# Attention scores and values in another layout, one transfer per q, k and v, and GpSimd's work of the first block given to VectorE

## The chip, the cores and the metric

The kernel runs on one NeuronCore of a Trainium2 chip. The metric is the device time of one execution in microseconds (us). Its engines are called by the names of the profile: PE (TensorE, matrix products; PEld is its weight loads), DVE (VectorE), ACT (ScalarE), POOL (GpSimd) and SP (SyncE, which issues the transfers here).

## The reference

Three stages follow each other. Local attention over chunks of 64 rows, then two feed-forward layers with different activations:

```python
B, H, S, D = q.shape                  # 4, 8, 576, 64
scores = scale * q_c @ k_c.T          # inside chunks of 64
attn = exp(scores - max) / (sum + 1e-9)
x = (attn @ v_c)  -> (B*S, H*D)       # 2304 tokens x 512
h = x @ w_in;  x = (h * sigmoid(1.702 * h)) @ w_out      # 512 -> 2048 -> 512
h = x @ w_in2; x = (h * tanh(softplus(h))) @ w_out2      # 512 -> 2048 -> 512
```

q, k and v are float32. The four weight matrices are float64, and the kernel reads them as pairs of 32-bit words.

## The kernel before, in words

**Tiling.** The 2304 tokens are 18 attention tiles of 128 tokens (two chunks of 64). Three tiles make a block of 384 tokens, so there are six blocks (j). The hidden width of 2048 is 16 slices (f). A step n is one slice of one block. In a step of the first layer `in_proj` (line 347) makes the hidden slice in 12 matrix products, ACT applies the activation (`gelu`, line 359), and `out_a` (line 374) adds the slice of two steps earlier to the block's output in 12 products.

**High and low parts.** Every product is made of three: each operand is split into a high part (the value rounded to the short form that PE reads fast) and a low part (the value minus its high part). `mm3` (line 342) multiplies high by high, high by low and low by high. So each weight piece, each hidden slice and each x needs one cast for the high part and one subtraction for the low part.

**Weights of the first layer.** There are 32 pieces of 512 KB (16 of w_in, 16 of w_out), in the order in which the first block needs them. Each goes through four operations, which `Weights` (lines 75 to 186) holds: `load` (SP, into one of 5 buffers), `scale` (ACT, line 141), `join` (DVE, lines 151 and 152, which make one float32 of two words), `split` (ACT casts the high part, line 173; POOL subtracts for the low part, line 174). A buffer can be filled again once the subtraction has read it. `convert` (line 177) does one of each for successive pieces, twice per step while the first block lasts. The pieces stay in memory for the other five blocks. The second layer's weights are joined during the first layer, written out, and split when the second layer begins, with the subtraction on POOL.

**Attention.** A tile goes through `load` (q, k, v), `transposes` (PE), copies of both (ACT or DVE), `scores` (PE), `shift` (DVE: maximum at line 277, subtraction at line 278), `exp` (ACT), `sums` (DVE, lines 291 to 293), `normalize` (line 297; POOL in the first block, DVE later), `attn_t` (PE), a copy (ACT), `pv` (PE), `x_hi` (ACT) and `x_lo` (DVE). `scores` and `pv` are 16 products of 64 by 64 per tile. They are placed on quarters of the 128 by 128 array: the partitions of the operands choose the rows, those of the result the columns. q and k come in two transfers per tile and v in four, so that two heads of a pair and two chunks lie where the products want them.

**Order.** All engines take their instructions in the order in which the program writes them. The first three tiles and steps 0 to 3 follow a list written by hand (`PLAN`, line 24): a letter is an operation, the number its tile or step. "w" is a number of idle products that keep PE busy. From step 4 on the loop at line 539 writes each step; in it tile 4 and tile 5 are made in the first block, one attention operation group per step. Within a step the order is `in_proj`, one `convert`, `gelu`, `g_hi`, `g_lo` (the hidden slice's own split; in the first block its subtraction is on POOL, line 370), attention, `out_a`, the other `convert`.

Of the kernel before, what the change touches and what calls it, by code (L numbers as in the profile page):

```python
# [9 lines left out]
F32 = mybir.dt.float32  # L10
F32R = mybir.dt.float32r
AF = mybir.ActivationFunctionType
ALU = mybir.AluOpType
# [3 lines left out]
P = 128  # L17
# [18 lines left out]
def tile_kernel(  # L36
# [40 lines left out]
    class Weights:  # L77
# [8 lines left out]
        def __init__(self, w_in, w_out, staged):  # L86
# [5 lines left out]
            self.raw, self.f32, self.hi, self.lo = {}, {}, {}, {}  # L92
            self.first, self.ahead = 0, NRAW - 2 if staged else NRAW
# [33 lines left out]
        def load_ahead(self):  # L127

            used = self.at["join" if self.staged is not None else "split"]
# [36 lines left out]
        def split(self):  # L166
# [7 lines left out]
            nc.gpsimd.tensor_tensor(out=lo, in0=w, in1=hi.bitcast(F32), op=ALU.subtract)  # L174
            self.hi[key], self.lo[key] = hi, lo

        def convert(self):
# [35 lines left out]
    def load_values(t, i):  # L213

        for c in range(2):
            b, s = divmod(i * P + c * CH, S)
            for r in range(2):
                nc.sync.dma_start(
                    out=t[r * CH : (r + 1) * CH].rearrange("k (p c d) -> k p c d", c=2, d=D)[:, :, c],
                    in_=v[b, r * NP : (r + 1) * NP, s : s + CH, :].rearrange("p k d -> k p d"),  # L220
                )

    class Attention:
# [31 lines left out]
        def scores(self):  # L255
            self.pt = pt = self.psum("sc")
            for p in range(NP):
                for c in range(2):
                    c0 = p * P + c * CH
                    cs = slice(c * CH, (c + 1) * CH)  # L260
                    for r in range(2):
                        rs = slice(r * CH, (r + 1) * CH)
                        nc.tensor.matmul(
                            pt[cs, r, p * CH : (p + 1) * CH],
                            self.qt[rs, c0 : c0 + CH],
# [191 lines left out]
    with tc.manual_schedule():  # L457
# [193 lines left out]
```

## Time and profile before

| what | us |
|---|---|
| median of 3 runs (lowest, highest) | 895.48 (894.75, 896.47) |
| the profiled execution's own time | 894.35 |
| its span in the profile | 892.4 |
| PE busy / DVE busy / ACT busy / POOL busy | 869.9 / 355.6 / 276.8 / 115.0 |

The span is the time from the first to the last recorded instruction. PE's busy time is the union of its matrix products, whose ends are modelled, so that products that overlap count once. Share of the span tells little here, because the first 110 us have another limit than the rest; the rows below are therefore taken by stretch.

### The profile page before, as it was taken

To read this page: it belongs to the slowest core of one execution; us is meant where nothing else is said; L and a number is where in the kernel's file an instruction comes from. 1 tells how busy PE (TensorE), PEld (TensorE's weight loads), DVE (VectorE), ACT (ScalarE), POOL (GpSimd) and SP (SyncE) were. 2 spreads that over 40 slices of the span, in tenths; PEclk is the share of its full clock that TensorE was granted. 3 is DMA by queue.
4 is the path that set the end of the run, shared out by engine and by line. 5 is a ranking of instruction groups with operands and counts; after the bars stand their busy time and mean duration, and the time that the engine had idled before them with its cause. 6 is when DMAs were issued, how large, how long until landed. Compare 5 with 4: busy or idle time off the path is not lost.

```text
span 892.4 us, 13796 instructions
## 1 busy us (share of the span) xinstructions
PE 869.9 (97%) x5724; PEld 812.1 (91%) x5724; DVE 355.6 (40%) x633; ACT 276.8 (31%) x469; POOL 115.0 (13%) x92
## 2 busy tenths in 40 slices
PE   7878999999999999999999999999999999999998
PEld 5777899999999999999999999999999999999997
DVE  5789744445445455445333222222222222222221
ACT  4777733333334343333434111111111111111111
POOL 2688700000000000000565000000000000000000
PEclk9999999999999999999999999999999999999999
DMA  8957724455336435523342000300200200200000
GB/s 208 284 163 218 213 96 107 107 139 181 117 96 195 125 107 169 153 71 128 112 127 83 1 1 1 107 1 1 106 1 1 107 1 1 107 1 1 36 1 36
DMA packets 93406, 82.69 MB, mean 93 GB/s; under 512 B 60320, under 2 KB 76704, under 8 KB 93344
## 3 DMA queue, kind: packets, MB, share of 16 engines
q1 hardware_dynamic: 93344, 81.81, 31.0%
q8 instruction: 45, 0.74, 0.3%
q14 instruction: 17, 0.14, 0.1%
HBM read 62.39 MB, written 19.40 MB: 92 GB/s over the span
## 4 chain that ended last, share of the span: by engine, by line
PE 88%; DVE 4%; DMA 3%; ACT 2%; SPq 2%; issue 1%; POOL 0%; DVEq 0%; POOLq 0%; ACTq 0%
PE h L345 14%; PE h L343 14%; PE h L344 14%; PE acc L343 7%; PE acc L344 6%; PE acc L345 6%; PE accb L435 5%; PE accb L434 5%; PE accb L433 5%; PE third L434 3%; PE third L435 2%; PE third L433 2%; DVE raw L152 2%; DVE raw L151 2%; PE tr L247 1%
## 5 line engine op out<-in xcount | busy, mean ns | idle before, releaser
L365 DVE CAST gh<-t 128x384 fp32r<-128x384 f32 x176 | 69.3, 394 | 476.0 <-ACT t L413 296.1
L343 PE MATMUL h<-xh,wi 128*128 128x384 f32 x512 | 172.0, 336 | 1.9 <-ACT t L361 1.8
L345 PE MATMUL h<-xh,wi 128*128 128x384 f32 x512 | 171.9, 336 | 0.6 <-POOL wi L174 0.6
L344 PE MATMUL h<-xl,wi 128*128 128x384 f32 x512 | 171.3, 335 | 0.0
L413 ACT ACTIVATE t<-h 128x384 f32<-128x384 f32 x96 | 47.2, 492 | 335.2 <-PE h L345 334.4
L343 PE MATMUL acc<-gh,wo 128*128 128x384 f32 x384 | 134.1, 349 | 0.0
L344 PE MATMUL acc<-gl,wo 128*128 128x384 f32 x384 | 128.6, 335 | 0.0
L345 PE MATMUL acc<-gh,wo 128*128 128x384 f32 x384 | 128.5, 335 | 0.0
L370 DVE TENSOR_TENSOR gl<-t,gh 128x384 fp32r<-128x384 f32 x176 | 98.3, 559 | 11.8
L361 ACT ACTIVATE t<-h 128x384 f32<-128x384 f32 x96 | 47.1, 491 | 172.3 <-PE h L345 81.3
L343 PEld LDWEIGHTS h<-xh,wi 128*128 128x128 f32 x512 | 96.1, 188 | 4.6 <-ACT t L361 3.2
L344 PEld LDWEIGHTS h<-xl,wi 128*128 128x128 f32 x512 | 96.1, 188 | 1.3
L345 PEld LDWEIGHTS h<-xh,wi 128*128 128x128 f32 x512 | 96.1, 188 | 0.9 <-POOL wi L174 0.9
L345 PE MATMUL h<-x2h,wi 128*128 128x384 f32 x256 | 86.4, 337 | 0.0
L343 PE MATMUL h<-x2h,wi 128*128 128x384 f32 x256 | 86.2, 337 | 0.0
L344 PE MATMUL h<-x2l,wi 128*128 128x384 f32 x256 | 86.0, 336 | 0.0
L435 PE MATMUL accb<-wo,gl 128*128 128x512 f32 x192 | 76.2, 397 | 0.0
L434 PE MATMUL accb<-wo,gh 128*128 128x512 f32 x192 | 75.8, 395 | 0.0
L433 PE MATMUL accb<-wo,gh 128*128 128x512 f32 x192 | 74.6, 389 | 0.0
L343 PEld LDWEIGHTS acc<-gh,wo 128*128 128x128 f32 x384 | 72.1, 188 | 2.0
L344 PEld LDWEIGHTS acc<-gl,wo 128*128 128x128 f32 x384 | 72.2, 188 | 0.0
L345 PEld LDWEIGHTS acc<-gh,wo 128*128 128x128 f32 x384 | 72.1, 188 | 0.0
(85 smaller groups left out, 1052.5 us busy)
## 6 DMA issues: line engine op xcount, KB each, us to landing
raw<-in_moe_w_in_dram SPq DMA_DIRECT2D x32, 512.0 KB, 4.1
raw<-in_moe_w_out_dram SPq DMA_DIRECT2D x32, 512.0 KB, 4.0
w_f<-wf SPq DMA_DIRECT2D x32, 256.0 KB, 2.2
ws<-w_f SPq DMA_DIRECT2D x32, 256.0 KB, 2.7
v<-in_v_dram SPq DMA_DIRECT2D x72, 64.0 KB, 2.9
out_dram<-o SPq DMA_DIRECT2D x18, 256.0 KB, 2.1
q<-in_q_dram SPq DMA_DIRECT2D x26, 128.0 KB, 4.2
k<-in_k_dram SPq DMA_DIRECT2D x26, 128.0 KB, 4.3
```

The lines of the kernel that those rows point to most:

```text
L151: nc.vector.tensor_scalar(lo, lo, 29, None, op0=ALU.logical_shift_right)
L152: nc.vector.scalar_tensor_tensor(to, hi, 3, lo, op0=ALU.logical_shift_left, op1=ALU.bitwise_or)
L343: nc.tensor.matmul(o, wh, mh, start=start, stop=False)
L344: nc.tensor.matmul(o, wh, ml, start=False, stop=False)
L345: nc.tensor.matmul(o, wl, mh, start=False, stop=stop)
L361: nc.scalar.activation(gt[n], hp.pop(n), AF.Gelu_apprx_sigmoid)
L365: (nc.scalar.copy if n < KF else nc.vector.tensor_copy)(gh[n], gt[n])
L370: eng.tensor_tensor(out=gl[n], in0=gt.pop(n), in1=gh[n].bitcast(F32), op=ALU.subtract)
L413: nc.scalar.activation(gt[n], h, AF.Mish)
L433: nc.tensor.matmul(o, a[:, ts], wh, start=f == 0, stop=False)
L434: nc.tensor.matmul(o, a[:, ts], wl, start=False, stop=False)
L435: nc.tensor.matmul(o, b[:, ts], wh, start=False, stop=f == KF - 1)
```

## The change

**Layout and transfers.** The heads now lie in q, k and v as they do in memory. So q, k and v of a tile are read in one transfer each (two where a tile crosses a batch). `scores` puts two neighbouring head pairs on the two halves of the result's partitions, and both chunks of a head pair side by side. `pv` takes the rows of the array by chunk and its columns by head; before, it took rows by head and columns by pair.

**Engines.** In the first layer's weights, in the hidden slices of the first block and in `normalize`, the subtraction or product that POOL did is now on DVE. POOL keeps the second layer's weights.

**Order.** A weight piece's subtraction is no longer written with its cast: it is put on a list (`open`) and written after the next piece's `join` (`rest`). A hidden slice's subtraction is written in the next step, before that step's `gelu`. `PLAN` is unchanged; its letter U now means DVE.

```diff
         def load_ahead(self):
-            used = self.at["join" if self.staged is not None else "split"]
+            used = self.at["join"] if self.staged is not None else self.at["split"] - len(self.open)
...
             nc.scalar.copy(hi, w)
-            nc.gpsimd.tensor_tensor(out=lo, in0=w, in1=hi.bitcast(F32), op=ALU.subtract)
-            self.hi[key], self.lo[key] = hi, lo
+            self.hi[key] = hi
+            self.open.append((key, w, hi, lo))
+            if self.staged is not None:
+                self.rest()
+
+        def rest(self):
+            eng = nc.vector if self.staged is None else nc.gpsimd
+            while self.open:
+                key, w, hi, lo = self.open.pop(0)
+                eng.tensor_tensor(out=lo, in0=w, in1=hi.bitcast(F32), op=ALU.subtract)
+                self.lo[key] = lo
+
+        def parts(self, key):
+            if key not in self.lo:
+                self.rest()
+            return self.hi[key], self.lo[key]
...
             if self.at["scale"] > self.at["join"]:
                 self.join()
+            self.rest()
             if self.at["load"] > self.at["scale"]:
                 self.scale()
...
-            for r in range(2):
-                nc.sync.dma_start(
-                    out=t[done : done + n].rearrange("t (p r d) -> t p r d", r=2, d=D)[:, :, r],
-                    in_=src[b, r * NP : (r + 1) * NP, s : s + n, :].rearrange("p t d -> t p d"),
-                )
+            nc.sync.dma_start(
+                out=t[done : done + n].rearrange("p (h d) -> p h d", h=H),
+                in_=src[b, :, s : s + n, :].rearrange("h p d -> p h d"),
+            )
...
-            self.v = at.tile([P, H * D], F32, tag="v", name=f"v{self.i}")
-            load_values(self.v, self.i)
+            self.v = load_tok(at, "v", v, self.i)
...
         def scores(self):
-            for p in range(NP):
+            for u in range(NP // 2):
                 for c in range(2):
-                    c0 = p * P + c * CH
-                    cs = slice(c * CH, (c + 1) * CH)
-                    for r in range(2):
-                        rs = slice(r * CH, (r + 1) * CH)
-                        nc.tensor.matmul(
-                            pt[cs, r, p * CH : (p + 1) * CH],
+                    o = (u * 2 + c) * CH
+                    for w in range(2):
+                        c0 = (2 * u + w) * P + c * CH
+                        for r in range(2):
+                            rs = slice(r * CH, (r + 1) * CH)
+                            nc.tensor.matmul(
+                                pt[w * CH : (w + 1) * CH, r, o : o + CH],
...
         def pv(self):
-                    w, o = p % 2, p // 2 * P + c * CH
-                    vs = slice((2 * p + c) * D, (2 * p + c + 1) * D)
-                    qs = slice(p * P + c * CH, p * P + (c + 1) * CH)
+                    cs = slice(c * CH, (c + 1) * CH)
                     for r in range(2):
-                        rs = slice(r * CH, (r + 1) * CH)
+                        h = 2 * p + r
+                        o = (r * NP // 2 + p // 2) * P + p % 2 * CH
                         nc.tensor.matmul(
-                            pt[w * D : (w + 1) * D, r, o : o + CH],
-                            self.v[rs, vs],
-                            self.a[rs, qs],
+                            pt[r * D : (r + 1) * D, c, p * CH : (p + 1) * CH],
+                            self.v[cs, h * D : (h + 1) * D],
+                            self.a[cs, o : o + CH],
...
     def g_lo(n):
-        eng = nc.gpsimd if n < KF else nc.vector
-        eng.tensor_tensor(out=gl[n], in0=gt.pop(n), in1=gh[n].bitcast(F32), op=ALU.subtract)
+        nc.vector.tensor_tensor(out=gl[n], in0=gt.pop(n), in1=gh[n].bitcast(F32), op=ALU.subtract)
...
-            "U": lambda i: tiles[i].normalize(pool),
-            "u": lambda i: tiles[i].normalize(nc.vector),
+            "U": lambda i: tiles[i].normalize(nc.vector),
...
                 if n < KF:
                     W[0].convert()
+                while late:
+                    g_lo(late.pop())
                 gelu(n)
                 g_hi(n)
-                g_lo(n)
+                if n < KF:
+                    late.append(n)
+                else:
+                    g_lo(n)
...
-                    att.normalize(pool if n < KF else nc.vector)
+                    att.normalize(nc.vector)
```

The order of instructions at three places. In these rows stands the line, the operation, what it writes and reads, and the size of the result; line numbers after the change are 1 to 16 higher than before.

The first place is DVE's queue while the first three tiles are finished, before step 0. raw is a weight piece, wi and wo its split parts, xl the low part of x, e the exponentials. Before:

```order
L151 TENSOR_SCALAR raw_221<-raw_221 128x512
L152 SCALAR_TENSOR_TENSOR raw_221<-raw_221 128x512
L339 TENSOR_TENSOR xl_387<-pv_315,xh_386 128x4x128
L151 TENSOR_SCALAR raw_273<-raw_273 128x512
L152 SCALAR_TENSOR_TENSOR raw_273<-raw_273 128x512
L339 TENSOR_TENSOR xl_387<-pv_348,xh_386 128x4x128
L339 TENSOR_TENSOR xl_387<-pv_398,xh_386 128x4x128
```

And after:

```order
L152 TENSOR_SCALAR raw_212<-raw_212 128x512
L153 SCALAR_TENSOR_TENSOR raw_212<-raw_212 128x512
L307 TENSOR_TENSOR e_201<-e_201,rc_237 128x512
L307 TENSOR_TENSOR e_first<-e_first,rc_275 128x512
L348 TENSOR_TENSOR xl_366<-pv_300,xh_365 128x2x4x64
L152 TENSOR_SCALAR raw_264<-raw_264 128x512
L153 SCALAR_TENSOR_TENSOR raw_264<-raw_264 128x512
L185 TENSOR_TENSOR wi_345<-raw_168,wi_345 128x512
L185 TENSOR_TENSOR wi_373<-raw_197,wi_373 128x512
L185 TENSOR_TENSOR wo_393<-raw_212,wo_393 128x512
L348 TENSOR_TENSOR xl_366<-pv_328,xh_365 128x2x4x64
L348 TENSOR_TENSOR xl_366<-pv_376,xh_365 128x2x4x64
```

The normalizing of tiles 1 and 2 (L307) now stands behind the joins of the first three pieces, and three pieces' subtractions (L185) stand ahead of the low parts of x of tiles 1 and 2.

The second place is one step of the loop in the first block. POOL's queue before, some two steps of it:

```order
L174 TENSOR_TENSOR wo_747<-raw_602,wo_747 128x512
L174 TENSOR_TENSOR wi_768<-raw_612,wi_768 128x512
L370 TENSOR_TENSOR gl_780<-t_776,gh_778 128x384
L174 TENSOR_TENSOR wo_818<-raw_652,wo_818 128x512
L174 TENSOR_TENSOR wi_839<-raw_685,wi_839 128x512
L370 TENSOR_TENSOR gl_851<-t_847,gh_849 128x384
```

DVE's queue after, one step:

```order
L152 TENSOR_SCALAR raw_624<-raw_624 128x512
L153 SCALAR_TENSOR_TENSOR raw_624<-raw_624 128x512
L185 TENSOR_TENSOR wo_719<-raw_583,wo_719 128x512
L152 TENSOR_SCALAR raw_626<-raw_626 128x512
L153 SCALAR_TENSOR_TENSOR raw_626<-raw_626 128x512
L185 TENSOR_TENSOR wi_740<-raw_624,wi_740 128x512
L378 TENSOR_TENSOR gl_748<-t_682,gh_684 128x384
```

All three of POOL's operations of a step now stand between the joins in DVE's queue; a piece's subtraction follows the join of the piece after it.

The third place is SP's queue at the start. Before:

```order
L207 DMA q_first<-in_q_dram 128x4x64 x2
L207 DMA k_first<-in_k_dram 128x4x64 x2
L110 DMA raw_174<-in_moe_w_in_dram 128x4x256
L110 DMA raw_203<-in_moe_w_in_dram 128x4x256
L218 DMA v_205<-in_v_dram 64x4x64 x4
L115 DMA raw_221<-in_moe_w_out_dram 128x1024
L110 DMA raw_273<-in_moe_w_in_dram 128x4x256
L218 DMA v_275<-in_v_dram 64x4x64 x4
L218 DMA v_299<-in_v_dram 64x4x64 x4
```

And after:

```order
L223 DMA q_first<-in_q_dram 128x8x64
L223 DMA k_first<-in_k_dram 128x8x64
L111 DMA raw_168<-in_moe_w_in_dram 128x4x256
L111 DMA raw_197<-in_moe_w_in_dram 128x4x256
L223 DMA v_199<-in_v_dram 128x8x64
L116 DMA raw_212<-in_moe_w_out_dram 128x1024
L111 DMA raw_264<-in_moe_w_in_dram 128x4x256
L223 DMA v_266<-in_v_dram 128x8x64
L223 DMA v_287<-in_v_dram 128x8x64
```

The order of the transfers is the same; the 28 issues up to the third tile's v (two further pairs of q and k ahead of these rows included) have become 13.

## Rows read from the trace of the kernel before

**Rows 1.** Windows: busy us (count) of PE, PEld, DVE, ACT, POOL; clock, DMA share, GB/s.

```profile
0.00:28.09 28.09, 20.94 (x272) 14.55 (x273) 15.94 (x30) 13.36 (x22) 7.15 (x12) 0.88 0.85 204
28.09:110.00 81.91, 70.35 (x540) 65.57 (x538) 71.07 (x73) 63.06 (x108) 64.11 (x47) 1.00 0.77 224
110.00:892.00 782.00, 778.62 (x4916) 732.01 (x4916) 268.57 (x531) 200.41 (x340) 43.74 (x35) 1.00 0.25 75
```

**Rows 2.** Groups of DVE, 28.09 to 110: busy us, mean ns | idle before.

```profile
L152 DVE SCALAR_TENSOR_TENSOR raw<-raw 128x512 int32<-128x512 int32 x28 | 36.6, 1306 | 3.2 <-ACT raw L141 0.9
L151 DVE TENSOR_SCALAR raw<-raw 128x512 int32<-128x512 int32 x28 | 28.3, 1011 | 1.8 <-DMA raw<-in_moe_w_in_dram 1.8
...
L291 DVE TENSOR_REDUCE sm<-e 128x8 f32<-128x512 f32 x3 | 2.0, 682 | 1.4 <-ACT e L286 1.4
...
L339 DVE TENSOR_TENSOR xl<-pv,xh 128x512 fp32r<-128x512 f32 x2 | 1.4, 684 | 1.6 <-ACT xh L335 1.6
```

**Rows 3.** Timeline of DVE, 78 to 82 and 98 to 102: start us, us, instruction.

```profile
78.08 0.42 DVE L151 TENSOR_SCALAR raw<-raw 128x512 int32<-128x512 int32 x1
78.61 0.69 DVE L152 SCALAR_TENSOR_TENSOR raw<-raw 128x512 int32<-128x512 int32 x1
79.21 1.25 DVE L151 TENSOR_SCALAR raw<-raw 128x512 int32<-128x512 int32 x1
80.57 1.60 DVE L152 SCALAR_TENSOR_TENSOR raw<-raw 128x512 int32<-128x512 int32 x1
...
98.21 0.68 DVE L277 TENSOR_REDUCE mx<-sc 128x8 f32<-128x512 f32 x1
...
101.36 0.39 DVE L151 TENSOR_SCALAR raw<-raw 128x512 int32<-128x512 int32 x1
```

**Rows 4.** Timeline of POOL, 78 to 82.

```profile
78.75 1.43 POOL L370 TENSOR_TENSOR gl<-t,gh 128x384 fp32r<-128x384 f32 x1 [1.13 <-ACT gh L365]
80.14 1.47 POOL L174 TENSOR_TENSOR wo<-raw,wo 128x512 fp32r<-128x512 f32 x1
```

**Rows 5.** Groups of DVE, whole span: busy us, mean ns of one | idle before.

```profile
L370 DVE TENSOR_TENSOR gl<-t,gh 128x384 fp32r<-128x384 f32 x176 | 98.3, 559 | 11.8
...
L297 DVE TENSOR_TENSOR e<-e,rc 128x512 f32<-128x512 f32 x12 | 8.3, 692 | 0.4
```

**Rows 6.** Timeline of the start, POOL, DVE and PE.

```profile
14.92 1.04 POOL L297 TENSOR_TENSOR e<-e,rc 128x512 f32<-128x512 f32 x1 [0.41 <-DVE rc L293]
...
16.13 1.04 PE L303 MATMUL at<-ident,e 128*128 128x128 f32 x8
...
19.69 1.59 PE L319 MATMUL pv<-a,v 64*64 64x64 f32 x32 [2.52 <-DMA v<-in_v_dram]
...
20.49 0.69 DVE L152 SCALAR_TENSOR_TENSOR raw<-raw 128x512 int32<-128x512 int32 x1
...
27.70 0.66 PE L247 MATMUL tr<-ident,k 128*128 128x128 f32 x4 [1.12 <-DMA k<-in_k_dram]
```

**Rows 7.** Timeline of SP's queue, 12 to 20.

```profile
12.81 7.17 SPq L218 DMA_DIRECT2D v<-in_v_dram  x8
```

**Rows 8.** Chain that ended last: start us, us, piece.

```profile
110.00 0.74 PE pv L319 x30
...
138.08 0.67 PE pv L319 x30
...
148.19 0.62 PE sc L263 x32
```

**Rows 9.** Timeline of PE and PEld, 138.9 to 139.4.

```profile
138.96 0.34 PE L344 MATMUL acc<-gl,wo 128*128 128x384 f32 x1
138.96 0.19 PEld L345 LDWEIGHTS acc<-gh,wo 128*128 128x128 f32 x1
...
139.14 0.35 PE L345 MATMUL acc<-gh,wo 128*128 128x384 f32 x1
```

**Rows 10.** Groups of PEld, whole span.

```profile
L319 PEld LDWEIGHTS pv<-a,v 64*64 64x64 f32 x544 | 11.5, 143 | 11.2 <-issue 5.7 <-ACT a L308 5.1 <-ACT xh L335 0.3
```

More of the change, by code (lines that the diff above doesn't have):

```diff
@@ L92, in __init__ @@
             self.raw, self.f32, self.hi, self.lo = {}, {}, {}, {}
+            self.open = []
             self.first, self.ahead = 0, NRAW - 2 if staged else NRAW
@@ L256, in scores @@
             self.pt = pt = self.psum("sc")
-            for p in range(NP):
+            for u in range(NP // 2):
                 for c in range(2):
-                    c0 = p * P + c * CH
-                    cs = slice(c * CH, (c + 1) * CH)
-                    for r in range(2):
-                        rs = slice(r * CH, (r + 1) * CH)
-                        nc.tensor.matmul(
-                            pt[cs, r, p * CH : (p + 1) * CH],
-                            self.qt[rs, c0 : c0 + CH],
-                            self.kt[rs, c0 : c0 + CH],
-                            start=True,
-                            stop=True,
-                        )
+                    o = (u * 2 + c) * CH
[5 more added lines that the diff above has]
+                                pt[w * CH : (w + 1) * CH, r, o : o + CH],
+                                self.qt[rs, c0 : c0 + CH],
+                                self.kt[rs, c0 : c0 + CH],
+                                start=True,
+                                stop=True,
+                            )
         def shift(self):
@@ L274, in shift @@
             self.eg = self.e.rearrange("p (g k) -> p g k", g=G)
-            sv = self.pt[:, :, 0 : NP * CH].rearrange("p r (h k) -> p r h k", h=NP)
-            mx = st.tile([P, 2, NP, 1], F32, tag="mx", name=f"mx{self.i}")
+            sv = self.pt[:, :, 0 : G // 2 * CH].rearrange("p r (g k) -> p r g k", k=CH)
+            mx = st.tile([P, 2, G // 2, 1], F32, tag="mx", name=f"mx{self.i}")
             nc.vector.reduce_max(out=mx, in_=sv, axis=AX.X)
             nc.vector.tensor_tensor(
-                out=self.e.rearrange("p (h r k) -> p r h k", h=NP, r=2),
+                out=self.e.rearrange("p (r g k) -> p r g k", r=2, k=CH),
                 in0=sv,
-                in1=mx.to_broadcast([P, 2, NP, CH]),
+                in1=mx.to_broadcast([P, 2, G // 2, CH]),
                 op=ALU.subtract,
@@ L332, in x_hi @@
             sl = slice(self.t * P, (self.t + 1) * P)
-            self.x = self.pt[:, :, 0 : NP * CH].rearrange("p r (a t) -> p r a t", t=P)
-            self.xo = [x[j][:, :, sl].rearrange("p (r a) t -> p r a t", r=2) for x in (xh, xl)]
+            self.x = self.pt[:, :, 0 : NP * CH].rearrange("p c (a t) -> p c a t", a=NP)
+            self.xo = [x[j][:, :, sl].rearrange("p a (c t) -> p c a t", c=2) for x in (xh, xl)]
             copy(self.xo[0], self.x)
@@ L348, in in_proj @@
         h = ps.tile([P, TB], F32, tag="h", name=f"h{f}")
-        a, b = w.hi["i", f], w.lo["i", f]
+        a, b = w.parts(("i", f))
         for kk in range(KD):
@@ L380, in out_a @@
         a, b = gh.pop(n), gl.pop(n)
-        wh, wl = W[0].hi["o", f], W[0].lo["o", f]
+        wh, wl = W[0].parts(("o", f))
         for m in range(KD):
@@ L482, in load_v @@
             tiles[i].v = half_slot(f"v{i}", w1.room(f"v{i}"))
-            load_values(tiles[i].v, i)
+            load_into(tiles[i].v, v, i)
         def keep_warm(n):
@@ L496, in split, with join @@
                 w1.load_ahead()
-        act, vec, pool = nc.scalar.copy, nc.vector.tensor_copy, nc.gpsimd
+        def join():
+            w1.join()
+            w1.rest()
+        act, vec = nc.scalar.copy, nc.vector.tensor_copy
         steps = {
@@ L504, in tile_kernel @@
             "c": lambda _: w1.scale(),
-            "j": lambda _: w1.join(),
+            "j": lambda _: join(),
             "s": lambda _: split(),
@@ L536, in tile_kernel @@
         att = tiles[TT]
-        nxt, done = tiles[TT + 1], 2
+        nxt, done, late = tiles[TT + 1], 2, []
         for n in range(4, N + LAG):
```

7 lines of the change are left out of this document (removed).

## The prediction, made before any run of the change

> **What bounds the kernel now.** I first read the windows, to see where PE has time to lose. From 110 us to the end PE is busy for 778.62 of 782.00 us [rows 1]. Nothing that happens on another engine there can buy time, and only a PE instruction that gets shorter or longer counts. From 28.09 us, where step 0 begins, to 110.00 us, where `pv` of tile 5 begins [rows 8], PE works for 70.35 of 81.91 us, so 11.6 us are to be had. In the same stretch DVE is busy for 71.07 us and POOL for 64.11 us. Before 28.09 us PE does little that counts.
>
> Next come the groups of that stretch [rows 2]. DVE's two join instructions take 36.6 + 28.3 = 64.9 us for 28 pieces, 2.3 us a piece. The timeline tells why [rows 3, 4]. POOL sat idle for 1.13 us before 78.75, and the pair that starts at 78.08 then took 0.42 and 0.69 us, and let the next instruction start at 79.21: 1.13 us for a piece. The pair behind it ran beside POOL's instructions of 78.75 and 80.14 and took 1.25 and 1.60 us. So DVE is the bound of this stretch, and more than half of its load is time spent against POOL. PE's loss follows from late DVE and ACT.
>
> **The change, part by part.** The sum is made for the profiled execution, 894.35 us (a span of 892.4 and 1.95 around it). The median of the runs is 1.13 us above it, which I add at the end.
>
> *DVE takes POOL's work, 28.09 to 110.* I add up start-to-start steps. An instruction of 0.69 us lets the next one start 0.60 later (78.61 to 79.21) [rows 3], so I take 0.09 us off each duration.
> - 28 joins with POOL silent, 28 × 1.13 = 31.6 us, in place of 64.9.
> - Weight subtractions. The new order has 32, three of them ahead of the low parts of x that step 0 needs, so 29 lie here. The trace has none on DVE. The nearest rows are the join's second half with two strided inputs (0.69) [rows 3], and the hidden slice's subtraction of 384 elements (559 ns) [rows 5], which gives 0.75 by its length for 512. I take 0.69, the row of the same size. 29 × 0.60 = 17.4 us; the other end adds 1.7.
> - Hidden slices' subtractions 0 to 13: 14 × 0.47 = 6.6 us (559 ns) [rows 5].
> - `normalize` of tiles 3 to 5: 692 ns [rows 5], 3 × 0.60 = 1.8 us.
> - What DVE did already: from a tile's maximum to the instruction behind its sums, 3.15 us with a wait of 0.70 in it [rows 3], two such waits making the 1.4 [rows 2], so 2.45 × 3 = 7.4 us; two low parts of x, 1.2 us.
>
> Together 66.0 us. DVE's named waits were 0.9 + 1.8 + 1.4 + 1.6 = 5.7 us [rows 2]. The 1.8 is a wait for a weight transfer behind the crowded start of SP's queue, which the change thins out; I drop it and keep 3.9. A check of the method on the kernel before: 64.9 + 7.4 + 1.2 + 5.7 = 79.2 of 81.91 us, so 2.7 are in no row, and they stay. 66.0 + 3.9 + 2.7 = 72.6 us. PE's own 70.35 us are so close to that that two engines which take instructions in order will wait for each other; I add 1.0 us for it, an estimate. That makes 73.6, a gain of 8.3 us. The ends: 11.6 where PE alone sets the pace, and 1.8 where DVE's waits double (66.0 + 11.4 + 2.7 = 80.1).
>
> *The start.* `normalize` of tile 1 ended on POOL at 15.96, and PE had transposed two tiles by 17.17 [rows 6]. Now it stands on DVE behind the third join, which ended at 21.18. Tile 0's `normalize` stands ahead of it too, and I let the joins that lose POOL's company pay for that. So tile 1 is ready near 21.8, and behind PE's wait for it stands `pv` of tile 0, which moves from 19.69 to about 22.4: 2.7 us later. It does not all come through. `pv` was already late by 2.52 us for v, and the transposes before step 0 waited 1.12 us for k of tile 3 [rows 6]. SP spent 7.17 us on eight issues of v [rows 7], which are now two, and k stands behind them, so this wait goes. ACT's copies and the cast of the first piece, queued behind tile 1, move with it, and three subtractions stand ahead of two low parts of x (1.8 us, partly inside DVE's wait for `pv`). I put step 0 at 1.0 us later: 0 if earlier transfers hide all, 3.0 if nothing but the wait for k is won back and PE, idle for longer, stays at its lower clock. The mean granted clock up to 28.09 us is 0.88 [rows 1], so PE has some time at the lower of its two levels there.
>
> *One subtraction a step later.* A buffer is asked for again when its subtraction is done. That was POOL's, which was behind; now it follows one join. At 73.6 us the DMA share of 0.77 becomes 0.86; the first 28 us ran at 0.85 [rows 1], so the transfers can do it, with little room. I cost it at nothing; what covers it is the time between asking for a piece and its scaling, and if that is gone the 1.8 us wait that I dropped comes back.
>
> *`scores` and `pv`.* `scores` keeps its sequence of array quarters: rows alternate with each product, columns with every second. I cost it at nothing. `pv` changes from rows first to columns first. It took 0.67 us from its first to the next product, `scores` 0.62 [rows 8]. Each on PE's path, 18 times: 0.05 × 18 = 0.9 us to win if it becomes like `scores`, and the rival below is the other end. I take 0, since both kinds of sequence now pass in about the same time.
>
> *Layout of the copies and the shift, fewer issues after the start:* nothing, since PE is the bound there and DVE works 268.57 of 782.00 us [rows 1]; without that cover it would be a changed stride in instructions of unchanged size.
>
> Sum: -8.3 + 1.0 = -7.3 us; 894.35 - 7.3 = 887.05, and the median 888.2.
>
> **The rivals.**
> - *PE becomes the bound.* All 11.6 us come back and the start costs nothing: 883.9. For it speaks that weights are prepared some steps ahead; against it that DVE's sum is only 2 us from PE's before any wait.
> - *DVE's new queue waits.* Subtractions wait for ACT's casts, and joins now stand behind them, as does the next tile's maximum, so PE gets tiles late. With the named waits doubled the gain is 1.8 - 1.0 = 0.8: 894.7, no change that can be seen. For it: ACT is busy for 63.06 of the 81.91 us [rows 1]. Against: casts come a join ahead of their subtraction.
> - *Slower: `pv` neighbours share rows.* Of the 16 products of a tile, 8 now follow one on the same rows of the array with other columns. If each such product waits for its weights, at 143 ns a load [rows 10], that is 8 × 0.143 × 18 = 20.6 us on PE's path: 888.2 + 20.6 = 908.8. It decides from 7.3 / 18 = 0.41 us per tile, three exposed loads. Against it: the load of 138.96 ran beside a product that used the same rows, all of them, and the next product started 0.18 us later [rows 9]. The Trainium skill, TensorE: Matmul & The Clock Gate, Part 3, says that a weight load overlaps with products in flight only when the row group differs, which would make this case the likely one. By the row above the trace does not agree for whole-array products; no run here shows it yet for quarters, and so the chance stays small.
> - *The change does not do what it says.* If POOL were not what slows the joins, 64.9 us would stay and 17.4 + 6.6 + 1.8 = 25.8 come on top: about 915. Against: the two pairs side by side [rows 3, 4].
>
> **How the numbers follow.** The forecast has 0.65, PE as bound 0.17, the waits 0.09, `pv` 0.06, the unchanged joins 0.03. A measurement of this kernel can tell about 0.2%, 1.8 us, from no change. Faster by more: the forecast but for its edge, and PE as bound, 0.82. Within: the waits and a little of the forecast, 0.09. Slower: 0.09. The range reaches down to PE as bound with `pv` like `scores`, 883.9 - 0.9, rounded to 882.5, and up to the waits, 894.5. The two cases beyond it have 0.09, and about 0.08 is left for both edges.
>
> **What would show it.** Right: join pairs of 0.42 and 0.69 us throughout the first 110 us; POOL silent until the second layer's weights; subtractions on DVE near 0.69; `pv` of tile 5 near 102.7 in place of 110.00 and from there the same distances; PE waiting for tile 1's `normalize` near 17 to 22 us. Wrong: joins still above 1 us; PE idle for `lo` parts in the first block; DVE waiting for transfers or casts for much more than 4 us; `pv` above 0.8 us in later blocks.

## The result, and the profile after

| | median, us | lowest to highest |
|---|---|---|
| the kernel before | 895.12 | 894.19 to 896.47 |
| the changed kernel | 885.39 | 884.17 to 886.77 |

The ratio is 0.9891, with a 95% interval of 0.987 to 0.9911: faster by 9.7 us. The forecast was 888.2, with 882.5 to 894.5 around it. The profiled execution took 884.17 us, its span is 882.4 us.

I cut every profile at the same two places: at the second product of step 0, from which PE can work without a pause (the first product alone may wait for its partner), and at the start of `pv` of tile 5, where PE becomes the only bound. The windows view of the changed kernel, with the columns of [rows 1] (the first stretch ends at the time at which that of [rows 1] did):

```profile
0.00:28.09 28.09, 19.49 (x273) 13.14 (x273) 17.68 (x35) 13.57 (x24) 0.70 (x6) 0.94 0.95 226
28.56:101.00 72.44, 68.86 (x535) 65.58 (x535) 64.29 (x120) 61.79 (x106) 0.00 (x0) 1.00 0.82 244
101.00:882.39 781.39, 777.70 (x4917) 731.30 (x4916) 268.85 (x532) 200.37 (x340) 40.73 (x32) 1.00 0.25 75
```

POOL is silent in the first block, as intended. PE is idle for 3.6 us of that stretch, where it had been for 11.6 [rows 1]. Cut at these two places, the 9.96 us by which the span is shorter come apart like this:

| part | before | after | difference | predicted |
|---|---|---|---|---|
| up to the second product | 28.37 | 28.56 | +0.19 | +1.0 |
| block: from there to `pv` of tile 5 | 81.63 | 72.44 | -9.19 | -8.3 |
| from there to the end | 782.35 | 781.39 | -0.96 | 0 |

The groups of DVE, 28.55 to 101.0, which answer to [rows 2]:

```profile
L153 DVE SCALAR_TENSOR_TENSOR raw<-raw 128x512 int32<-128x512 int32 x28 | 19.4, 694 | 2.1
L152 DVE TENSOR_SCALAR raw<-raw 128x512 int32<-128x512 int32 x28 | 11.8, 422 | 0.0
L185 DVE TENSOR_TENSOR wo<-raw,wo 128x512 fp32r<-128x512 f32 x15 | 10.2, 687 | 1.9 <-ACT wo L174 1.8
L185 DVE TENSOR_TENSOR wi<-raw,wi 128x512 fp32r<-128x512 f32 x14 | 9.6, 685 | 0.0
L378 DVE TENSOR_TENSOR gl<-t,gh 128x384 fp32r<-128x384 f32 x15 | 8.2, 553 | 1.1 <-ACT gh L374 1.1
...
L301 DVE TENSOR_REDUCE sm<-e 128x8 f32<-128x512 f32 x3 | 2.1, 684 | 1.4 <-ACT e L296 1.4
L348 DVE TENSOR_TENSOR xl<-pv,xh 128x512 fp32r<-128x512 f32 x2 | 1.4, 692 | 1.0 <-ACT xh L344 1.0
```

The join pair fell from 1011 and 1306 ns [rows 2] to 422 and 694, the two prices that the forecast took. The four waits on the right make 5.3 us; before they made 5.7. In a second profile of the same kernel (after_again, below) they made 7.3, 3.6 of them for `wo`.

The start, from the timeline of DVE and PE, which answers to [rows 6] (in brackets, how long the engine was idle before the instruction and what ended that):

```profile
20.19 0.69 DVE L307 TENSOR_TENSOR e<-e,rc 128x512 f32<-128x512 f32 x1
...
21.02 0.63 PE L313 MATMUL at<-ident,e 128*128 128x128 f32 x4 [4.72 <-DVE e L307]
21.57 1.07 PE L328 MATMUL pv<-a,v 64*64 64x64 f32 x32
...
27.19 0.42 PE L352 MATMUL h<-xh,wi 128*128 128x384 f32 x1
...
28.56 0.44 PE L353 MATMUL h<-xl,wi 128*128 128x384 f32 x1 [0.95 <-DVE xl L348]
```

PE waits 4.72 us for tile 1's `normalize` behind the joins, and `pv` of tile 0 moves from 19.69 [rows 6] to 21.57. Behind it time is won back, so that the second product is only 0.19 us later. In the second profile it is 0.96 us later. The two differ in PE's granted clock: up to 28.09 us its mean is 0.94 in the first and 0.88 in the second, and 0.88 in the kernel before [rows 1].

### The profile page after: what moved, and what is told of

It reads as the page before. It is cut to its first block, busy times and chain, and to the rows that moved or that the text cites. A ratio compares the mean times of both kernels' runs of the same rounds, so it can differ in the third digit from the quotient of the medians.

```text
span 882.4 us, 13567 instructions
## 1 busy us (share of the span) xinstructions
PE 866.1 (98%) x5724; PEld 810.0 (92%) x5724; DVE 351.3 (40%) x687; ACT 276.2 (31%) x469; POOL 41.4 (5%) x38
## 4 chain that ended last, share of the span: by engine, by line
PE 89%; DVE 5%; ACT 3%; DMA 2%; issue 0%; SPq 0%; DVEq 0%; ACTq 0%
PE h L354 14%; PE h L352 14%; PE h L353 14%; PE acc L352 7%; PE acc L353 7%; PE acc L354 7%; PE accb L443 5%; PE accb L442 5%; PE accb L441 5%; PE third L442 3%; PE third L443 3%; PE third L441 2%; PE tr L256 1%; DVE raw L153 1%; DMA raw<-in_moe_w_in_dram 1%; PE sc L273 1%
## 5 line engine op out<-in xcount | busy, mean ns | idle before, releaser
L378 DVE TENSOR_TENSOR gl<-t,gh 128x384 fp32r<-128x384 f32 x192 | 107.1, 558 | 13.2 <-ACT gh L374 1.1
L352 PEld LDWEIGHTS acc<-gh,wo 128*128 128x128 f32 x384 | 72.2, 188 | 2.0
```

Of the source, the lines that this page charges most:

```text
L352: nc.tensor.matmul(o, wh, mh, start=start, stop=False)
L378: nc.vector.tensor_tensor(out=gl[n], in0=gt.pop(n), in1=gh[n].bitcast(F32), op=ALU.subtract)
```

## The experiments

All of them are cut at the same two places. "Rest" is from `pv` of tile 5 to the end of the span.

| kernel | median (lowest to highest) | ratio to before, 95% | start | block | rest |
|---|---|---|---|---|---|
| the change | 885.39 (884.17 to 886.77) | 0.987 to 0.9911 | 28.56 | 72.44 | 781.39 |
| layout_only | 890.5 (890.07 to 891.14) | 0.9935 to 0.9968 | 25.98 | 80.83 | 781.41 |
| engines_only | 890.03 (888.91 to 891.32) | 0.9931 to 0.996 | 28.97 | 76.90 | 782.38 |
| pool_busy | 903.71 (903.46 to 904.48) | 1.0084 to 1.0115 | 30.03 | 91.25 | 781.42 |
| no_later | 903.61 (902.61 to 904.47) | 1.0081 to 1.0112 | 33.17 | 86.70 | 781.43 |
| more_transfers | 890.39 (889.37 to 892.31) | 0.992 to 0.9966 | 29.84 | 77.33 | 781.46 |
| g_at_once | 887.97 (886.8 to 889.25) | 0.9887 to 0.9945 | 28.91 | 74.72 | 781.40 |
| u_early | 883.36 (882.64 to 885.42) | 0.9837 to 0.9889 | 27.27 | 73.35 | 781.39 |
| pv_rows_first | 885.81 (885.14 to 886.07) | 0.9862 to 0.9909 | 29.16 | 72.73 | 781.48 |
| x_first | 883.65 (883.0 to 884.06) | 0.9863 to 0.9892 | 26.08 | 74.37 | 781.40 |
| after_again | 885.82 (884.84 to 886.51) | 0.9881 to 0.9917 | 29.33 | 73.94 | 781.41 |
| pv_cols_by_four | 886.56 (one run) | none | 29.49 | 72.93 | 782.33 |

The rest is alike to 0.1 us in all kernels with the same sequence of columns in `pv` (below). The start and the block are not: the change's own second profile (after_again) has 0.8 us more in the first and 1.5 us more in the second. So differences of single blocks count here only where they are well above that, or where the waits that make them can be named.

**Half of the change each: the layout with its transfers, and the engines with their order.**

```diff
# layout_only: the change, with POOL's work given back and nothing written later
-            if self.staged is not None:
-                self.rest()
+            self.rest()
...
-            eng = nc.vector if self.staged is None else nc.gpsimd
+            eng = nc.gpsimd
...
+        eng = nc.gpsimd if n < KF else nc.vector
+        eng.tensor_tensor(out=gl[n], in0=gt.pop(n), in1=gh[n].bitcast(F32), op=ALU.subtract)
...
-            "U": lambda i: tiles[i].normalize(nc.vector),
+            "U": lambda i: tiles[i].normalize(nc.gpsimd),
...
-                if n < KF:
-                    late.append(n)
-                else:
-                    g_lo(n)
+                g_lo(n)
# engines_only: the kernel before, with open, rest, late and DVE, but its own layout and transfers
```

Expected of layout_only: 

> The change's layout, transfers, scores and pv; the subtractions and normalize of the first block stay on GpSimd and in their old place. Theory (GpSimd slows VectorE's joins, and the gain is their return to 0.42 and 0.69 us): joins stay at about 1.0 and 1.3 us on average, and of the 9.7 us gained only pv's 0.9 and up to 1.5 us of the start come: 893, between 891.5 and 894.5. Rival (the transfers and the layout bring the gain): 887 or less.

Expected of engines_only: 

> The kernel before with its layout and transfers, but VectorE in GpSimd's place in the first block and the subtractions one step later, as in the change. Theory: joins at 0.42 and 0.69 us, 886 to 889, the rest of the way to 885.4 being pv's 0.9 us and the start. Rival (transfers and layout): 893 or more.

Both missed. The layout brought 4.6 us in place of about 2, and the engines alone 5.0 in place of 6 to 9. With the layout alone the joins stay slow. The groups of DVE in its block:

```profile
L153 DVE SCALAR_TENSOR_TENSOR raw<-raw 128x512 int32<-128x512 int32 x28 | 37.8, 1349 | 2.9 <-ACT raw L142 0.5
L152 DVE TENSOR_SCALAR raw<-raw 128x512 int32<-128x512 int32 x28 | 28.9, 1032 | 0.3 <-DMA raw<-in_moe_w_in_dram 0.3
```

Its gain is made elsewhere: 2.4 us at the start, 0.8 in the block and 0.9 in the rest. (How much of the 2.4 the transfers made is not shown; see the part on the prediction.) With the engines alone the joins have the change's prices, but DVE waits for 10.0 us in the block where the change waits for 5.3, and that difference of 4.7 is the difference between their blocks (76.90 and 72.44: 4.5). Against the change's second profile (7.3 and 73.94) it is 2.7 and 3.0, so its size is known only within these bounds. The two halves do not simply add up in the block: the layout with its transfers brings 0.8 us there beside slow joins, and 3.0 to 4.5 us on top of the engines and the order. The two groups of DVE that hold most of it:

```profile
L152 DVE TENSOR_SCALAR raw<-raw 128x512 int32<-128x512 int32 x28 | 11.8, 423 | 0.8 <-DMA raw<-in_moe_w_in_dram 0.8
L185 DVE TENSOR_TENSOR wo<-raw,wo 128x512 fp32r<-128x512 f32 x15 | 10.2, 687 | 6.0 <-ACT wo L174 6.0
```

**Is it the number of transfers?** The change with its layout, engines and order, but q and k in two transfers and v in four, by halves of the heads and of the rows.

```diff
+        rows = 2 if src is v else 1
...
-            nc.sync.dma_start(
-                out=t[done : done + n].rearrange("p (h d) -> p h d", h=H),
-                in_=src[b, :, s : s + n, :].rearrange("h p d -> p h d"),
-            )
+            for lo in range(0, n, n // rows):
+                e = lo + n // rows
+                for r in range(2):
+                    hs = slice(r * NP, (r + 1) * NP)
+                    nc.sync.dma_start(
+                        out=t[done + lo : done + e].rearrange("p (h d) -> p h d", h=H)[:, hs],
+                        in_=src[b, hs, s + lo : s + e, :].rearrange("h p d -> p h d"),
+                    )
```

Expected of more_transfers: 

> The changed kernel with q and k of a tile in two transfers each and v in four, as many as in the kernel before; layout, engines and order stay the change's. Theory (SP's queue): each issue stands ahead of the weight pieces on SP's queue, pieces come later, ACT's casts and so DVE wait; this is what the engines-and-order-alone kernel lacked: 889.5 us (888 to 891), the stretch from step 0 to pv of tile 5 near 77 us in place of 72.4, DVE's waits for ACT's weight casts near 6 us in place of 1.8. Rival (the new layout of scores, shift and pv brings it, the number of transfers nothing): 885 to 886.5.

The theory held: 890.39, 5.0 us above the change (4.6 above its second group of runs, after_again), and the block is 77.33. DVE waits 10.4 us in it, 5.8 of them for `wo`, where the change waits for `wo` 1.8 us in one profile and 3.6 in the other:

```profile
L185 DVE TENSOR_TENSOR wo<-raw,wo 128x512 fp32r<-128x512 f32 x15 | 10.2, 687 | 5.9 <-ACT wo L174 5.8
```

SP's queue shows the place. First the change, around the issues for one tile:

```profile
59.47 0.39 SPq L223 DMA_DIRECT2D q<-in_q_dram  x1
59.91 0.57 SPq L223 DMA_DIRECT2D k<-in_k_dram  x1
60.53 2.87 SPq L223 DMA_DIRECT2D v<-in_v_dram  x1
63.50 0.88 SPq L111 DMA_DIRECT2D raw<-in_moe_w_in_dram  x1
```

The same tile with eight issues:

```profile
63.26 0.93 SPq L228 DMA_DIRECT2D q<-in_q_dram  x2
64.24 1.05 SPq L228 DMA_DIRECT2D k<-in_k_dram  x2
65.33 4.86 SPq L228 DMA_DIRECT2D v<-in_v_dram  x4
70.29 0.55 SPq L111 DMA_DIRECT2D raw<-in_moe_w_in_dram  x1
```

The next weight piece is asked for 4.0 us behind the tile's first issue in the one, 7.0 us in the other. What follows from that, in the timeline of ACT and DVE of the second kernel:

```profile
74.62 0.68 ACT L142 ACTIVATE raw<-raw 128x512 f32<-128x512 f32 x1 [1.76 <-DMA raw<-in_moe_w_in_dram]
...
78.22 0.69 DVE L185 TENSOR_TENSOR wo<-raw,wo 128x512 fp32r<-128x512 f32 x1 [2.12 <-ACT wo L174]
```

ACT stands at the scaling of that piece, the cast behind it is late, and DVE waits 2.12 us, the longest wait of its block. Both kernels have their three longest waits of the block at the same places, in front of `wo`: near 35, 78 and 105 us here (1.65, 2.12 and 2.08 us), near 35, 77 and 104 us in engines_only (1.65, 2.01 and 2.08 us). In more_transfers PE's granted clock was 0.50 for 3.4 us twice in the block besides, which engines_only, with a block of nearly the same length, had not; so that is not what the 5.0 us are.

**Is POOL what slowed the joins?** The change, with three subtractions of 128 by 192 on POOL per weight piece of the first layer, whose result nobody reads.

```diff
                 self.lo[key] = lo
+                if self.staged is None:
+                    z = zeros.bitcast(F32)
+                    for c in range(3):
+                        x = hi[:, c * 128 : c * 128 + 192].bitcast(F32)
+                        nc.gpsimd.tensor_tensor(out=z, in0=x, in1=x, op=ALU.subtract)
```

Expected of pool_busy: 

> The change, and in addition three GpSimd subtractions of 128x192 per weight piece of the first layer, which read the finished high part and write a tile that nobody reads. No instruction waits for them. Theory (the two engines stand in each other's way at the memory): joins go back up by some 0.8 us a piece, and as VectorE sets the pace that is about 28 x 0.8 = 22 us: 907, between 897 and 912. Rival (GpSimd was slow in the chain of waits, and idle or busy does not matter to VectorE): 885 to 887.

903.71: the time lies in the theory's range, and the rival fell. The price was another than the theory had: a pair of joins rose by 0.32 us (829 + 610 ns for 694 + 422), not by 0.8, and the subtractions, which the theory left out, brought the rest. The window of its block (columns as in [rows 1]) and the groups of DVE in it:

```profile
30.03:121.28 91.25, 76.03 (x535) 71.35 (x535) 85.28 (x120) 62.30 (x105) 64.35 (x92) 0.91 0.66 193
```

```profile
L153 DVE SCALAR_TENSOR_TENSOR raw<-raw 128x512 int32<-128x512 int32 x28 | 23.2, 829 | 2.1
L152 DVE TENSOR_SCALAR raw<-raw 128x512 int32<-128x512 int32 x28 | 17.1, 610 | 0.0
L185 DVE TENSOR_TENSOR wi<-raw,wi 128x512 fp32r<-128x512 f32 x14 | 13.6, 969 | 0.0
L185 DVE TENSOR_TENSOR wo<-raw,wo 128x512 fp32r<-128x512 f32 x15 | 12.9, 867 | 0.0
L383 DVE TENSOR_TENSOR gl<-t,gh 128x384 fp32r<-128x384 f32 x15 | 12.5, 836 | 0.2 <-ACT gh L379 0.2
...
L293 DVE TENSOR_TENSOR e<-sc,mx 128x512 f32<-128x512 f32 x3 | 2.1, 692 | 0.1
L306 DVE TENSOR_REDUCE sm<-e 128x8 f32<-128x512 f32 x3 | 2.1, 684 | 1.4 <-ACT e L301 1.4
...
L353 DVE TENSOR_TENSOR xl<-pv,xh 128x512 fp32r<-128x512 f32 x2 | 1.4, 680 | 0.0
```

Not every DVE instruction pays. Joins and the subtractions for weights and hidden slices cost 0.14 to 0.28 us more each; the subtractions that read a result of PE (`sc`, `pv`) and the reductions cost what they did in the change. DVE was busy for 85.28 us in place of 64.29, 21.0 more, and its waits, 5.3 us in the change, shrank to 1.6; the kernel is 18.3 us slower than the change.

POOL was busy for 64.35 us in this block, as long as in the kernel before (64.11 [rows 1]). But that kernel lost more to it: its joins alone took 64.9 us [rows 2], 33.7 more than the change's 31.2. So POOL's busy time alone does not set the price. POOL's instructions were 92 of 128 by 192 here and 47 of 128 by 384 or 512 there; which property of them counts, no run shows. That pool_busy is still 8.6 us slower than the kernel before fits the work that DVE carries here besides.

**Is the later order needed?** Both subtractions in their own place, and then only the hidden slices'.

```diff
# no_later
-            if self.staged is not None:
-                self.rest()
+            self.rest()
...
# no_later and g_at_once
-                if n < KF:
-                    late.append(n)
-                else:
-                    g_lo(n)
+                g_lo(n)
```

Expected of no_later: 

> The change, but each subtraction is written right behind its cast again, ahead of the next join, and a hidden slice's in its own step. Theory (VectorE takes its instructions in order): it now waits for the cast on ScalarE, 0.6 us and what stands ahead of it, at most pieces: 2 to 5 us slower than the change, 887 to 890. Rival (the casts come early enough, the later place does nothing): 885.4 within 0.2%.

Expected of g_at_once: 

> The changed kernel with the weights' subtractions still a step later, but the hidden slices' subtraction in its own step. Theory (the 0.7 us that DVE stood still for nearly every weight piece in the kernel with nothing later was the weights' part, 29 pieces against 15 slices): most of the 18 us stays won, 886 to 890, DVE's waits for gh 3 to 6 us. Rival (both subtractions count alike, per wait): 15/44 of 18.2 us is lost, 891 to 893.

no_later missed by far: 903.61, slower than the kernel before. Its groups of DVE, 33.2 to 119.8:

```profile
L184 DVE TENSOR_TENSOR wo<-raw,wo 128x512 fp32r<-128x512 f32 x15 | 10.3, 687 | 7.7 <-ACT wo L174 7.7
L184 DVE TENSOR_TENSOR wi<-raw,wi 128x512 fp32r<-128x512 f32 x13 | 9.0, 691 | 8.6 <-ACT wi L174 8.6
L377 DVE TENSOR_TENSOR gl<-t,gh 128x384 fp32r<-128x384 f32 x15 | 8.3, 554 | 2.6 <-ACT gh L373 2.6
```

No price changed, only the right column: 18.9 us of waits in place of the 2.9 that these three lines have in the change. The spans of the two profiles differ by 18.9 us, of which 14.3 lie in the block and 4.6 in the start, where DVE waits 5.6 us for ACT's casts of w_in pieces, with the low parts of x behind them. One piece in the timeline:

```profile
61.68 0.69 DVE L153 SCALAR_TENSOR_TENSOR raw<-raw 128x512 int32<-128x512 int32 x1
...
62.41 0.65 ACT L174 CAST wi<-raw 128x512 fp32r<-128x512 f32 x1 [1.24 <-DVE raw L153]
...
63.09 0.69 DVE L184 TENSOR_TENSOR wi<-raw,wi 128x512 fp32r<-128x512 f32 x1 [0.71 <-ACT wi L174]
```

DVE and ACT wait for each other in turn: ACT 1.24 us for the join, DVE 0.71 us for the cast. With the subtraction behind the next join both have something to do meanwhile. g_at_once shows which of the two lists it is: 887.97, within the theory's 886 to 890, 2.6 us above the change, with this line for the hidden slices in its block:

```profile
L378 DVE TENSOR_TENSOR gl<-t,gh 128x384 fp32r<-128x384 f32 x15 | 8.3, 555 | 5.4 <-ACT gh L374 5.4
```

So of the 18.2 us the weights' part is about 15.6 and the slices' 2.6. The 2.6 is the less certain of the two: the change's own medians lie 0.4 us apart, and its second block (73.94) only 0.8 us below this one (74.72), but the wait of 5.4 us stands for 1.1 and 1.2 in the change's two profiles.

**`pv`'s sequence.** Its 16 products in other orders, with the change's operands and places.

```diff
# pv_rows_first: rows alternate with each product, columns with every second
-                for c in range(2):
-                    cs = slice(c * CH, (c + 1) * CH)
-                    for r in range(2):
+                for r in range(2):
+                    for c in range(2):
+                        cs = slice(c * CH, (c + 1) * CH)
...
# pv_cols_by_four: rows alternate with each product, columns with every fourth, as before
-            for p in range(NP):
-                for c in range(2):
+            for u in range(NP // 2):
+                for r, w, c in [(r, w, c) for r in range(2) for w in range(2) for c in range(2)]:
+                    p = 2 * u + w
```

Expected of pv_rows_first: 

> The changed kernel with pv's 16 products of a tile in the order in which the array's rows alternate with each product, as the kernel before had them; operands, places and results stay. Theory (sequences of quarters cost the same or 0.05 us a tile): 885.4 to 886.3, pv to the next product 0.62 to 0.67 us. Rival (a neighbour on the same rows exposes its weight load, and the change's sequence pays that): 0.62 would fall below 0.55, and the time to 884 or less.

Expected of pv_cols_by_four: 

> The changed kernel with pv's 16 products in an order in which the columns of the array stay for four products while the rows alternate, the kernel before's sequence; operands and places stay the change's. Theory (the 0.05 us a tile that pv lost hang on columns that stay for four products): 0.67 us from pv to the next product, from the second block on, and 886.3. Rival (they hung on where the operands lie or on the strides): 0.62, 885.4.

The timeline of PE in the second block, first the change, then pv_cols_by_four (the trace has two records for each of the 16 products, hence x32):

```profile
152.76 0.69 PE L328 MATMUL pv<-a,v 64*64 64x64 f32 x32
153.39 0.45 PE L352 MATMUL acc<-gh,wo 128*128 128x384 f32 x1
```

```profile
154.33 0.74 PE L328 MATMUL pv<-a,v 64*64 64x64 f32 x32
155.00 0.44 PE L352 MATMUL acc<-gh,wo 128*128 128x384 f32 x1
```

From `pv` to the next product it is 0.62 us (0.63 between these rounded rows) and 0.67. pv_rows_first has 0.62 too, and 885.81. So the change's neighbours on the same rows cost nothing (its rival fell), and the kernel before paid 0.05 us a tile for keeping the same columns over four products. The rest says the same over the whole run: 782.33 with that sequence (one run), 782.35 and 782.38 in the two kernels with the old `pv`, 781.39 to 781.48 in all others.

**The start.** The change lost little there in the sum, but PE waits in it. u_early moves `normalize` of tiles 1 and 2 ahead of the first three joins. x_first does that too, asks for v in the order of the tiles, and puts the low parts of x of tiles 1 and 2 ahead of all subtractions of weights but one. Of `PLAN`, shortened, the lines that differ:

```diff
# u_early
-... U0 c N1 c M2 j w17 l v0 A0 X2 N2 V0 c c j j v1 l U1 U2 A1 ...
+... U0 c N1 U1 c M2 j w17 l v0 A0 X2 N2 U2 V0 c c j j v1 l A1 ...
# x_first: J joins, r subtracts one piece
-... l v2 M1 ... U0 c N1 c M2 j w17 l v0 A0 X2 N2 V0 c c j j v1 l U1 U2 A1 ...
+... l v0 M1 ... U0 c N1 U1 c M2 j w17 l v1 A0 X2 N2 U2 V0 c c j j v2 l A1 ...
-... T3 j H2 d4 K3 L1 Q3 s L2 c j I0 ...
+... T3 L1 J r H2 L2 d4 K3 Q3 s r r c j I0 ...
```

Expected of u_early: 

> The changed kernel with normalize of tiles 1 and 2 directly behind their own sums on DVE, so ahead of the first three joins; nothing else is moved. Theory (PE's 4.7 us of waiting for tile 1 were that normalize behind the joins): the wait goes, pv of tile 0 starts near 19.5 in place of 21.6, step 0 near 26.0 to 27.0 in place of 28.6, and since DVE sets the pace of the block by its sum, which starts as much earlier, all comes through: 883 (882 to 884.5). Rival (joins moved behind two instructions make the first weight pieces late, or the block's pace is set by the transfers): step 0 not earlier than 28 or pv of tile 5 still at 101, 885 to 886.

Expected of x_first: 

> The changed kernel with normalize of tiles 1 and 2 behind their own sums, v asked for in the order of the tiles (0, 1, 2), and the low parts of x of tiles 1 and 2 ahead of the three first subtractions of weights but one. Theory (with the normalize moved, PE's 1.73 us wait for v and its 1.73 us wait for xl are what is left of the start): pv of tile 0 near 18.5, the second product of step 0 near 25.5 in place of 28.56, the block from there as long as in the changed kernel (72.4), so 882 (881 to 883.5). Rival (an earlier start finds the weight pieces later, or PE's clock lower behind the idle start, as the 0.52 us products of the first variant showed): block of 74 or more, 883.5 to 885.5.

Expected of after_again: 

> The changed kernel itself, beside the variant of its start on the same chip: 885.4 (884.5 to 886.5), by every theory.

The timeline of PE in u_early:

```profile
16.32 1.04 PE L313 MATMUL at<-ident,e 128*128 128x128 f32 x8
19.09 0.69 PE L328 MATMUL pv<-a,v 64*64 64x64 f32 x32 [1.73 <-DMA v<-in_v_dram]
...
27.27 0.45 PE L353 MATMUL h<-xl,wi 128*128 128x384 f32 x1 [1.73 <-DVE xl L348]
```

Its theory held in the time (883.36) and in the wait: the 4.72 us are gone and `pv` of tile 0 starts 2.5 us earlier, but only 1.3 of them reach the second product, since the low parts of x still stand behind three subtractions; so not all of it came through, as the theory had it. x_first reaches the second product at 26.08, 2.5 us ahead of the change, and its block is 74.37. Its windows:

```profile
26.08:36.50 10.42, 8.23 (x74) 7.60 (x74) 8.37 (x16) 9.28 (x17) 0.00 (x0) 0.99 1.06 374
36.50:39.90 3.40, 3.40 (x13) 3.40 (x12) 3.33 (x7) 2.87 (x5) 0.00 (x0) 0.50 1.15 165
39.90:100.45 60.55, 58.62 (x453) 56.18 (x451) 53.10 (x101) 50.92 (x88) 0.00 (x0) 1.00 0.75 218
```

PE ran out of weights near 34 us (it waited 2.19 us for a low part of `wi`; in the change 1.18), and then its granted clock was 0.50, the lower of its two levels, for 3.4 us. In u_early it was 0.50 from 27.6 to 31.0 us. So both things that the rival of x_first names, late weights and the lower clock, were there, and the time, 883.65, lies just above the theory's range, at the rival's lower edge. But the change's second profile has a block of 73.94 with a clock of 1.00 throughout, so that these two made x_first's block longer is not shown. x_first is 2.2 us below the change in the same group of runs (883.65 and 885.82, and the highest run of the one lies under the lowest of the other). u_early at 883.36 cannot be told from x_first; its highest run, 885.42, lies within the change's range.

## Why the prediction came out right, point by point

*POOL as the cause, DVE as the bound.* Shown, by pool_busy and by the joins' prices in every kernel where POOL is silent. The Trainium skill, SBUF — State Buffer, Who interferes with whom, says that a DVE instruction contends with a GpSimd instruction that reads SBUF where it has two inputs in SBUF, and with GpSimd where it runs in a two-port mode, and that reductions never do on this chip. The groups of pool_busy agree: `xl` and the `e` of L293, which read one input from PSUM, and the reductions are unchanged (680 to 692 ns), and the instructions with two inputs in SBUF are 0.14 to 0.28 us slower. The first join (L152) has one input in SBUF and is 0.19 us slower; whether it runs in a two-port mode no run here shows.

*The sum of DVE.* DVE was busy for 64.29 us of the block. The right column of its groups, the short ones that are left out above included, holds 7.9 us, 5.3 of them named waits and 2.6 steps from one instruction to the next. So the work is 66.9 where the forecast had 66.0, the waits are 5.3 where it had 3.9, and 66.9 + 5.3 = 72.2 of 72.44 us. The forecast's other two terms, 2.7 us that stood in no row and 1.0 us for engines that wait for each other, found nothing to pay for. In the change's second profile the block was 73.94, which is what the forecast had (73.6), so this size is right to about 1 us and no better. In part it is luck: the forecast took over the old waits, and engines_only shows that with the old transfers they would have been 10.0 us.

*The dropped wait.* "The 1.8 is a wait for a weight transfer behind the crowded start of SP's queue, which the change thins out; I drop it." It went, and another 1.8 (3.6 in the second profile), for ACT's cast of `wo`, came. But how much hung on SP's queue the forecast did not see: with as many transfers as before, DVE's waits rise to 10.4 us and 5.0 us of the 9.7 are gone. The forecast gave DVE's work the whole gain of the block; engines_only got 4.7 of it, where the sum without the dropped 1.8 gives 6.5. What failed is the cost of nothing for "fewer issues after the start". It looked only behind 110 us. Three tiles (4 to 6) are loaded inside the block, and their issues stand ahead of weight pieces on SP's queue.

*One subtraction a step later.* "I cost it at nothing" priced what the order might cost in buffers, and that was nothing. It did not price what it is for: without it the same work on DVE is 18.2 us slower than with it, and 8.5 slower than the kernel before. The sum held because it took DVE's old waits and added none for casts, which is true only in this order. The rival "DVE's new queue waits" named the mechanism and doubled the waits (11.4 us); in no_later the casts alone made 18.9.

*The start.* The mechanism was as put (PE's wait, 4.72 us, `pv` at 21.57 for a forecast of 22.4, DVE's three subtractions ahead of the low parts of x), and the size was +0.19 for +1.0 in one profile and +0.96 in the other. The forecast had earlier transfers cover the rest, and that is shown only in part. The wait for k of tile 3 shrank, where the forecast let it go (0.19 and 0.30 us in the change's two profiles and 0.99 in pv_rows_first, which starts alike; 1.12 before). In layout_only, which has the new transfers and not DVE's new queue, the second product is at 25.98, 2.4 us earlier than before. But `pv` of tile 0 starts only 0.46 us earlier there (19.23 for 19.69), behind a wait for v of 2.49 us, as long as before (2.52). Behind it PE's granted clock differs. First the kernel before, then layout_only, with the columns of [rows 1]:

```profile
19.49:26.32 6.83, 6.32 (x106) 4.99 (x106) 4.00 (x7) 4.83 (x9) 1.55 (x3) 0.50 0.78 184
```

```profile
19.23:25.12 5.89, 3.83 (x108) 2.87 (x109) 5.75 (x9) 4.67 (x9) 3.33 (x3) 1.00 1.14 288
```

The three `pv` take 0.69 us each there where they took 1.19 to 1.59, and the clock of 0.50 comes later, from 25.12 to 28.53. So what the start gains from fewer issues and what from the clock is not told apart here.

*`pv`.* Taken at 0 with 0.9 us to win at the other end; the other end came, 0.96 us in the rest (13 tiles lie in it, so 0.07 a tile by this measure, 0.05 by the rows of `pv`). The slower rival fell: eight products of a tile follow one on the same rows, and the tile takes 0.62 us either way. The Trainium skill, TensorE: Matmul & The Clock Gate, Part 3, has weight loads overlap products in flight only where the row group differs; for these quarters, as for the whole array [rows 9], the trace does not agree.

*The rivals.* PE as the bound came close (3.6 us of idle time left in the block). Joins that stay slow fell with the first profile. (Their "about 915" does not follow from the sum as written: 895.48 + 25.8 is 921.)

## What to carry to other kernels

Before work is moved from one engine to a busier one, see whether the first engine's work is what makes the second one slow: some 26 us of work came to DVE here (25.8 by the forecast's rows), and the block still became shorter, by 4.7 us with the old layout and transfers and by 9.2 us with the new ones. Then give each subtraction that waits for another engine's cast a place behind other work of its own queue; without that the move would have lost. And count the issues that stand ahead of the weights on one transfer queue: the bytes were the same, and the number of transfers was worth 5.0 us.

## What the runs showed that I had not expected

Beside POOL, a DVE instruction's price depends on what it reads: with 64 us of POOL work in the block, 829 ns for 694 and 969 for 685 where both inputs lie in SBUF, 680 for 692 where one comes from PSUM, and 684 for 684 in a reduction. And the same busy time of POOL cost DVE 33.7 us in the kernel before, in the joins alone, and 21.0 us in pool_busy.

Eight issues of q, k and v held SP for 6.9 us (63.26 to 70.19) where three held it for 3.9 (59.47 to 63.40), with the same bytes.

PE paid 0.05 us in a tile's 16 quarter products for keeping the same columns of the array over four of them; how its rows alternate made no difference.
